# Transposing Q by DMA instead of on TensorE, in a fused attention and gated convolution kernel

## The chip, the cores and the metric

One core of a Trainium2 chip. The metric is the device time of one execution in microseconds. Times of a kernel are medians of several executions. Each run also has a profile, whose "span" is shorter than the time of the same execution (the profiled run of the kernel before took 229.07 us). The engines are TensorE (PE, with its weight loads PEld), VectorE (DVE), ScalarE (ACT), GpSimd (POOL) and SyncE (SP), which here issues every DMA. Ratios are computed as the mean time of one kernel's fast runs over that of the other's fast runs in the same rounds, so they are not quite the ratio of the medians quoted. In the experiments they leave out the profiled run; where that run was the fastest, slow runs are in the ratio, and the text says so. A single execution has the state "unknown" and no interval; such runs are used only where the difference is tens of microseconds.

## The reference

```python
B, H, S, D = 8, 8, 576, 64
scores = q @ k^T / sqrt(D)                       # per batch and head
cum    = cumsum(max(s, 0))                       # decay bias, per key and query
scores = where(causal, -1e9, scores + min(-(cum_q - cum_k), 0))
attn   = softmax(scores) @ v                     # -> x of shape (B, S, 512)
gate   = sigmoid(causal depthwise conv of x, 5 taps)
out    = (gate * (x @ w_val)) @ w_out
```

q, k and v are float32 with entries of about 0.1, so the scores are small.

## The kernel before

The kernel is one long list of tasks. A planner, run when the kernel is built, gives each task an engine and a place in that engine's queue, from a table of priorities (`DUE`), a table of engine choices (`CHOICE`) and assumed durations. Each engine then works through its own queue in that order. The scores need Q and K with the head dimension on the partitions, so both are loaded, cast to bf16 on GpSimd, transposed on TensorE into PSUM and copied out again by ScalarE or VectorE. Partition p of a load holds rows 4p to 4p+3, because that makes runs of 1 KB; the copy out of PSUM puts the rows in order again.

```python
def dma_qk(b, which, hs, dst):
    nc.sync.dma_start(out=dst, in_=src[b, hs, 0:512, :].rearrange("h (p j) d -> p h (j d)", j=4))

def qk_T(b, p):                                   # TensorE: 4 transposes of Q, 4 of K, for 2 heads
    for which in range(2):
        for j in range(4):
            nc.tensor.transpose(pt[:, which, j * 128:(j + 1) * 128],
                                qkbs[which][b % 2][:, j, p * 128:(p + 1) * 128], ident)

def qk_evac(e, b, p):                             # ACT or DVE, rows back in order
    copy[e](QKTs[b % 2][:, :, p, 0:512].rearrange("d w (x j) -> d w x j", j=4), ...)

def tap(n, sh):                                   # one convolution tap on VectorE, 4 of these per channel group
    nc.vector.scalar_tensor_tensor(gp[:, sh:S], x[:, 0:S - sh], cwT[:, c, 4 - sh:5 - sh], gp[:, sh:S], ALU.mult, ALU.add)

# in the planner, for every SyncE task:
if e == "SP":
    idle_at[e] = now + 0.06                       # SyncE is taken to be free again after 0.06 us
    dma_free = max(dma_free, now + 1.2) + us      # the DMA engines are busy for `us`
```

Of the kernel before, what the change touches and what calls it, by code (L numbers as in the profile page):

```python
# [9 lines left out]
FP32 = mybir.dt.float32  # L10
# [9 lines left out]
NKB = 5  # L20
# [184 lines left out]
def pcol(kb, qb):  # L205
    if kb == qb:
        return kb * 128
    if qb == 4:
# [16 lines left out]
DUE = dict(w=-9.02, lwv=-0.69, lwo=-0.63, cwv=-14.48, cwo=12.35, av=1.54, norm=-21.42, xt=-10.52, xe=-5.49,  # L225
           tap=4.19, dtap=-0.1, tanh=-21.1, val=6.51, dval=0.82, out=13.05, dout=0.32, oute=12.26,
           qt=-3.29, qe=62.47, tt=-0.65, te=-32.14, s4=-6.89, vp=-31.92, cast=41.14, lqk=-6.48,
           mask=-32.97, lv=-68.98)

STAY = (0.33, 20.6)  # L230

CHOICE = dict(cast="22212012",
              wts="00",
              te="10100110",
              qe="10010001000100000100100000000000",
              xe="01000110000001000110100110101101",
              tap0="10200210102212220121120122002000",
              oute="1010000010101000001000010000100000100000")


class Plan:
# [3 lines left out]
    LAG = 0.2  # L245
    SWITCH = 0.18
# [16 lines left out]
    def run(self):  # L263
# [33 lines left out]
        while len(self.order) < len(self.tasks):  # L297
            started, later = False, []
            for e in engs:
                if idle_at[e] > now + 1e-9:  # L300
                    later.append(idle_at[e])
                    continue
                pick = None
                for t in ready[e]:
                    at = can(t)
                    if at is None:
                        continue
                    if at > now + 1e-9:
                        later.append(at)
                        continue  # L310
                    key = t["key"] + (STAY[t["mode"] == "N"] if e == "PE" and t["mode"] != mode else 0)
                    if pick is None or (key, t["n"]) < pick[:2]:
                        pick = (key, t["n"], t)
                if pick is None:
                    continue
                t = pick[2]
                us = t["us"]
                if e == "PE" and t["mode"] != mode:
                    us += self.SWITCH
                    mode = t["mode"]  # L320
                for kind, tok in t["take"]:
                    if kind == "bank":

                        got = max((bank[i ^ 1], -i) for i in range(8) if bank[i] <= now + 1e-9)
                        self.slot[kind, tok] = i = -got[1]
                        bank[i] = NEVER
                    elif kind == "pair":
                        got = min((max(bank[i], bank[i + 1]), i) for i in range(0, 8, 2))
                        self.slot[kind, tok] = i = got[1]
                        bank[i] = bank[i + 1] = NEVER  # L330
                    else:
                        got = min(free[kind])
                        free[kind].remove(got)
                        self.slot[kind, tok] = got[1]
                t["start"] = now
                if e == "SP":
                    idle_at[e] = now + 0.06
                    dma_free = max(dma_free, now + 1.2) + us
                    t["done"] = dma_free + 0.8
                else:  # L340
                    idle_at[e] = t["done"] = now + us
                for kind, tok in t["give"]:
                    i, at = self.slot[kind, tok], t["done"] + self.LAG
                    if kind in ("bank", "pair"):
                        bank[i:i + (2 if kind == "pair" else 1)] = [at] * (2 if kind == "pair" else 1)
                    else:
                        free[kind].append((at, i))
                ready[e].remove(t)
                self.order.append(t)
                later.append(idle_at[e])  # L350
                started = True
                for o in after[t["n"]]:
                    o["at"] = max(o["at"], t["done"] + (self.LAG if o["eng"] != e else 0.0))
                    o["left"] -= 1
                    if o["left"] == 0:
                        ready[o["eng"]].append(o)
            if not started:
                assert later
                now = min(later)
# [3 lines left out]
def main_path(ctx, tc, q, k, v, s, moe_w_val, moe_conv_w, moe_w_out, out, okcnt):  # L363
# [39 lines left out]
    make_identity(nc, identf)  # L403
    vst = one.tile([128, NKB, 8, 65], FP32, name="vst")
# [14 lines left out]
    glus = two("glu", [128, 4, S], BF16)  # L419
    sp = one.tile([64, S], FP32, name="sp")  # L420
# [37 lines left out]
    for m, (nm, src, dst, sc) in enumerate((("wv", moe_w_val, wv, 1.0), ("wo", moe_w_out, wo, 0.5))):  # L458
# [3 lines left out]
        t = add("SP", 3.6, DUE["l" + nm], load, take=[("qkf", nm)])  # L462
# [57 lines left out]
    def qk_T(b, p):  # L520
        pt = slot["qt", b, p] = bank(("qt", b, p), 128, 1024, BF16).rearrange("d (w s) -> d w s", w=2)
        for which in range(2):
            for j in range(4):
                nc.tensor.transpose(pt[:, which, j * 128:(j + 1) * 128],  # L524
                                    qkbs[which][b % 2][:, j, p * 128:(p + 1) * 128], ident)

    def qk_evac(e, b, p):
        copy[e](QKTs[b % 2][:, :, p, 0:512].rearrange("d w (x j) -> d w x j", j=4),  # L528
                       slot["qt", b, p].rearrange("d w (j x) -> d w x j", j=4))
# [33 lines left out]
    def mask(n, hh):  # L563
        d = slot["Pt", n][:, hh, 0:512].rearrange("k (g q) -> k g q", g=4)
        nc.gpsimd.affine_select(out=d, in_=d, pattern=[[0, 4], [1, 128]], compare_op=ALU.is_ge, fill=0.0, base=0,  # L565
                                channel_multiplier=-1)
# [15 lines left out]

    def norm(n):
        b, p = divmod(n, 4)
        pv = slot["av", n][:, :, 0:NKB * 65].rearrange("t h (g d) -> t h g d", d=65)
        nc.vector.reciprocal(recs[:, n], pv[:, :, :, 64])
# [3 lines left out]
    def x_T(n):  # L590
        b, p = divmod(n, 4)
        pt = slot["x", n] = bank(("x", n), 128, S, BF16)
        slot["g", n] = work("gp", n, [128, S], FP32)
        for i in (4, 0, 1, 2, 3):
            nc.tensor.transpose(pt[:, WIN[i]:WIN[i] + 128], xns[b % 2][:, i, p * 128:(p + 1) * 128], ident)  # L595
# [4 lines left out]

    def tap0(e, n):
        b, c = divmod(n, 4)
        scaled(e, slot["g", n], xTs[b % 2][:, c, :] if e == "POOL" else slot["x", n], cwT[:, c, 4:5])
# [39 lines left out]
    for b in range(B):  # L643
# [3 lines left out]
        if b == 0:  # L647
            t_tl = add("SP", 1.6, -8.4, lambda: load_tail(0))
            t_tail = T["tailc", 0] = add("DVE", 0.45, -6, lambda: nc.vector.tensor_copy(tailbs[0], tails[0]), [t_tl])
            for p in range(4):  # L650
                for wh in range(2):
# [3 lines left out]
                    t = add("SP", 0.95, -8.5 + 0.5 * p + wh * 0.01, ld)  # L655
                    T["cast", 0, wh, p] = add(("DVE", "ACT", "POOL"), (0.32, 0.5, 0.8), p - 9, lambda e, p=p, wh=wh: cast_qk(
                        copy[e], 0, wh, HP[p], slot["f", 0, wh, p]), [t], pick=("cast", 2 * p + wh))
                t = add("SP", 1.4, -8.3 + 0.5 * p, lambda p=p: load_v_pair(p))
                T["vp", 0, p] = add("DVE", 0.85, p - 2, lambda p=p: vprime(nc.vector, 0, p), [t, t_w])
        else:  # L660
            fs = []
            for wh in range(2):
                def ld(b=b, wh=wh):
                    f = slot["f", b, wh] = work("qkf", (b, wh), [128, 8, 256], FP32)
                    dma_qk(b, wh, slice(0, 8), f)
                t = add("SP", 3.8, n0 + DUE["lqk"], ld, take=[("qkf", (b, wh))])
                c = add("POOL", 1.95, n0 + DUE["cast"], lambda b=b, wh=wh: cast_qk(
                    nc.gpsimd.tensor_copy, b, wh, slice(0, 8), slot["f", b, wh]),
                    [t] + [T.get(("qt", b - 2, p)) for p in range(4)], give=[("qkf", (b, wh))])
                for p in range(4):  # L670
                    T["cast", b, wh, p] = c
            t = add("SP", 1.6, n0 + DUE["lqk"] + 0.5, lambda b=b: load_tail(b), [T.get(("tailc", b - 2))])
            t_tail = T["tailc", b] = add("POOL", 0.7, n0 + DUE["cast"] + 0.3, lambda b=b: nc.gpsimd.tensor_copy(
                tailbs[b % 2], tails[b % 2]), [t, T.get(("tt", b - 2))])
            ts = [add("SP", 1.7, n0 + DUE["lv"] + i * 0.01, lambda b=b, i=i: load_v_block(b, i),
                      [T["vp", b - 1, p] for p in range(4)]) for i in range(NKB)]
            for p in range(4):
                T["vp", b, p] = add("POOL", 1.4, n0 + p + DUE["vp"], lambda b=b, p=p: vprime(nc.gpsimd, b, p),
# [7 lines left out]
        for p in range(4):  # L686
            t = T["qt", b, p] = add("PE", 0.45, n0 + p + DUE["qt"] if b else p - 6.9, lambda b=b, p=p: qk_T(b, p),
                                    [T["cast", b, 0, p], T["cast", b, 1, p]] + old_s, take=[("bank", ("qt", b, p))])
            T["qe", b, p] = add(("ACT", "DVE"), (0.9, 1.15), n0 + p + DUE["qe"] if b else p - 6.8,
                                lambda e, b=b, p=p: qk_evac(e, b, p), [t], give=[("bank", ("qt", b, p))], pick=("qe", n0 + p))  # L690

        e4 = {}
        for ps_ in ([[p] for p in range(4)] if b == 0 else [[0, 1, 2, 3]]):
# [3 lines left out]
                [t_te] + [T["qe", b, p] for p in ps_] + [T.get(("av", b - 2, p)) for p in range(4)],  # L697
# [6 lines left out]
        for p in range(4):  # L704
            n = n0 + p
            es = []
            for i in range(3):
                take = [("pair", ("s", n, i))] + ([("P", n)] if i == 0 else [])
                t = T["s", n, i] = add("PE", 0.26, n + 0.3 * i, lambda n=n, i=i: scores(n, i),
                                       [T["qe", b, p], t_te if i else None, T.get(("s", n, i - 1)), T.get(("s", n - 1, 2))],  # L710
                                       take=take, mode="R")
                t = add("ACT", 0.905, n + 0.3 * i, lambda n=n, i=i: exps(n, i), [t], give=[("pair", ("s", n, i))])
                es += [t] if i else [add("POOL", 0.58, n + DUE["mask"] + 0.01 * hh, lambda n=n, hh=hh: mask(n, hh), [t])
# [5 lines left out]
            t = T["norm", n] = add("DVE", 0.94, n + DUE["norm"], lambda n=n: norm(n), [t], give=[("pair", ("av", n))])  # L719
# [5 lines left out]
            t = T["tap0", n] = add(("ACT", "DVE", "POOL"), (0.63, 0.73, 1.55), n + DUE["tap"],  # L725
                                   lambda e, n=n: tap0(e, n), [t, t_cw], pick=("tap0", n))
            for sh in range(1, 5):
# [15 lines left out]
        for i in range(NKB):  # L743
# [6 lines left out]
            add("SP", 0.95, n0 + DUE["oute"] + DUE["dout"] * i, lambda b=b, i=i: store(b, i), [t], give=[("ot", (b, i))])  # L750
# [81 lines left out]
```

## Time and profile before

| | before |
|---|---|
| time, median | 228.57 us (228.2 to 228.89) |
| span | 227.2 us |
| DVE / ACT / PE / POOL busy | 192.5 / 176.2 / 174.9 / 138.6 us |
| DMA queue's share of 16 engines | 66.7% |
| mean granted TensorE clock | 0.985 |

An engine's busy time is a lower bound for the span; what is above it is idle time, and the question is always which engine has least of it, and where. The lines themselves are shown in the prediction. One view is SyncE's own queue. These lines are its timeline over one batch in the middle of the kernel before. Columns: start, time from the first issue of the row to the end of its last, engine and line, operation, data, number of DMAs.

```profile
103.63 5.35 SPq L507 DMA_DIRECT2D vst<-in_v_dram  x5
109.08 0.56 SPq L482 DMA_DIRECT2D qkf<-in_q_dram  x1
109.74 1.02 SPq L482 DMA_DIRECT2D qkf<-in_k_dram  x1
110.85 1.44 SPq L482 DMA_DIRECT2D qkf<-in_q_dram  x1
113.44 4.59 SPq L641 DMA_DIRECT2D out_dram<-ot  x3
```

On average SyncE has room: its 129 issues sum to 111.5 us of 227. But 42.0 us of these fall in the first 45 us; from 80 to 210 us they are 45.8 us of 130.

### The profile page before, as it was taken

To read this page: it belongs to the slowest core of one execution; us is meant where nothing else is said; L and a number is where in the kernel's file an instruction comes from. 1 tells how busy PE (TensorE), PEld (TensorE's weight loads), DVE (VectorE), ACT (ScalarE), POOL (GpSimd) and SP (SyncE) were. 2 spreads that over 40 slices of the span, in tenths; PEclk is the share of its full clock that TensorE was granted. 3 is DMA by queue.
4 is the path that set the end of the run, shared out by engine and by line. 5 is a ranking of instruction groups with operands and counts; after the bars stand their busy time and mean duration, and the time that the engine had idled before them with its cause. 6 is when DMAs were issued, how large, how long until landed. Compare 5 with 4: busy or idle time off the path is not lost. (4 is left out here: it accounts for less than half of the span.)

```text
span 227.2 us, 5999 instructions
## 1 busy us (share of the span) xinstructions
PE 174.9 (77%) x2392; PEld 117.6 (52%) x2411; DVE 192.5 (85%) x319; ACT 176.2 (78%) x229; POOL 138.6 (61%) x154
## 2 busy tenths in 40 slices
PE   0777667768576987798877988896998999999750
PEld 0555453455443664467545654675566555656320
DVE  3546989699999597999999899999999999999900
ACT  2395989954598599985999979899999799966330
POOL 5374574599264995799987876885945775200000
PEclk9999996999999999999999999999999999999996
DMA  4999889999996299907994683159229123034351
GB/s 137 245 278 305 245 160 258 315 228 207 312 307 166 60 196 364 301 12 173 233 346 178 137 246 114 41 130 153 92 95 220 50 83 94 3 132 157 128 190 35
DMA packets 69230, 40.48 MB, mean 178 GB/s; under 512 B 47109, under 2 KB 63493, under 8 KB 69194
## 3 DMA queue, kind: packets, MB, share of 16 engines
q1 hardware_dynamic: 69194, 40.01, 66.7%
q8 instruction: 21, 0.34, 0.7%
q14 instruction: 15, 0.12, 0.2%
HBM read 30.57 MB, written 9.44 MB: 176 GB/s over the span
## 5 line engine op out<-in xcount | busy, mean ns | idle before, releaser
L609 DVE SCALAR_TENSOR_TENSOR gp<-banks,cwT,gp 128x575 f32<-128x575 bf16 (+3 forms) x128 | 103.5, 812 | 3.2 <-ACT gp L395 0.3
L559 ACT ACTIVATE P<-banks 128x1024 bf16<-128x1024 f32 x96 | 95.1, 1030 | 11.7 <-PE banks L533 11.1
L565 POOL TENSOR_SCALAR_AFFINE_SELECT P<-P 128x512 bf16<-128x512 bf16 x64 | 40.4, 653 | 36.4 <-ACT P L559 36.2
L533 PE MATMUL banks<-QKT 64*128 64x128 bf16 (+4 forms) x576 | 39.5, 250 | 15.6 <-ACT P L559 6.3
L621 PE MATMUL banks<-xT,wv 128*128 128x288 bf16 x256 | 40.6, 288 | 5.0 <-DVE gp L609 3.0
L633 PE MATMUL banks<-wo,glu 128*128 128x512 bf16 x141 | 37.6, 379 | 4.7 <-DVE glu L627 1.1
L580 PE MATMUL banks<-Vp,P 128*128 128x65 bf16 x960 | 35.8, 196 | 2.8 <-POOL Vp L495 1.3
L580 PEld LDWEIGHTS <-P 128*128 128x128 bf16 x960 | 33.7, 99 | 6.4 <-issue 3.3
L533 PEld LDWEIGHTS <-QKT 64*128 64x128 bf16 x576 | 19.2, 97 | 31.7 <-issue 25.6
L495 POOL TENSOR_TENSOR Vp<-vst,w 128x650 bf16<-128x650 f32 x28 | 35.3, 1282 | 0.0
L621 PEld LDWEIGHTS <-wv 128*128 128x128 bf16 x256 | 23.0, 98 | 17.1 <-issue 10.3
L528 ACT COPY QKT<-banks 128x1024 bf16<-128x1024 bf16 x26 | 26.1, 1019 | 5.4 <-PE banks L524 5.1
L627 DVE SCALAR_TENSOR_TENSOR glu<-th,banks 128x288 bf16<-128x288 f32 x64 | 27.1, 447 | 3.2 <-PE banks L621 2.7
L614 ACT ACTIVATE th<-gp 128x576 f32<-128x576 f32 x32 | 22.1, 692 | 9.2 <-DVE gp L609 9.0
L587 DVE TENSOR_TENSOR xn<-banks,recs 128x640 bf16<-128x640 f32 x32 | 26.4, 825 | 1.1
L638 ACT COPY ot<-banks 128x512 f32<-128x512 f32 (+1 forms) x31 | 18.1, 587 | 9.6 <-PE banks L633 6.0
L397 POOL TENSOR_SCALAR gp<-xT,cwT 128x576 f32<-128x576 bf16 x12 | 20.7, 1725 | 7.3 <-ACT xT L599 4.1
L633 PEld LDWEIGHTS <-glu 128*128 128x128 bf16 x160 | 14.6, 97 | 18.2 <-issue 5.0
L595 PE MATMUL banks<-ident,xn 128*128 128x128 bf16 x160 | 14.6, 223 | 6.3 <-DVE gp L609 2.8
L595 PEld LDWEIGHTS <-xn 128*128 128x128 bf16 x160 | 9.9, 99 | 12.7 <-DVE xn L587 5.0
L524 PE MATMUL banks<-ident,qb 128*128 128x128 bf16 x128 | 13.2, 230 | 2.1 <-DVE glu L627 0.7
L485 POOL CAST qb<-qkf 128x2048 bf16<-128x2048 f32 x7 | 13.2, 1891 | 2.3 <-DMA qkf<-in_q_dram 2.3
(56 smaller groups left out, 148.5 us busy)
## 6 DMA issues: line engine op xcount, KB each, us to landing
out_dram<-ot SPq DMA_DIRECT2D x32, 256.0 KB, 2.1
qkf<-in_q_dram SPq DMA_DIRECT2D x7, 1024.0 KB, 9.3
qkf<-in_k_dram SPq DMA_DIRECT2D x7, 1024.0 KB, 8.8
vst<-in_v_dram SPq DMA_DIRECT2D x28, 256.0 KB, 5.0
vst<-in_v_dram SPq DMA_DIRECT2D x15, 128.0 KB, 4.5
first<-in_q_dram SPq DMA_DIRECT2D x4, 256.0 KB, 3.3
first<-in_k_dram SPq DMA_DIRECT2D x4, 256.0 KB, 3.5
tail<-in_q_dram SPq DMA_DIRECT2D x8, 128.0 KB, 8.8
```

What stands on the lines that cost most here:

```text
L495: eng.tensor_tensor(Vps[b % 2][:, :, h], vst[:, :, h], w[:, :, b * 8 + 2 * p:b * 8 + 2 * p + 2].unsqueeze(3).to_broadcast([128, NKB, 2, 65 ...
L528: copy[e](QKTs[b % 2][:, :, p, 0:512].rearrange("d w (x j) -> d w x j", j=4), slot["qt", b, p].rearrange("d w (j x) -> d w x j", j=4))
L533: nc.tensor.matmul(ps[:, hh, c0:c0 + nq], QKTs[b % 2][r, 1, p, k0:k0 + 128], QKTs[b % 2][r, 0, p, q0:q0 + nq], **kw)
L559: nc.scalar.activation(out=slot["Pt", n][:, :, step * 512:(step + 1) * 512], in_=slot["s", n, step], func=AF.Exp, scale=0.125)
L565: nc.gpsimd.affine_select(out=d, in_=d, pattern=[[0, 4], [1, 128]], compare_op=ALU.is_ge, fill=0.0, base=0, channel_multiplier=-1)
L580: nc.tensor.matmul(ps[:, hh, qb * 65:qb * 65 + 65], lhsT, Vps[b % 2][:, kb, 2 * p + hh, :], start=(kb == 0), stop=(kb == qb))
L587: nc.vector.tensor_tensor(xns[b % 2][:, :, p * 128:(p + 1) * 128].rearrange("t g (h d) -> t h g d", h=2), pv[:, :, :, 0:64], recs[:, n].un ...
L595: nc.tensor.transpose(pt[:, WIN[i]:WIN[i] + 128], xns[b % 2][:, i, p * 128:(p + 1) * 128], ident)
L609: nc.vector.scalar_tensor_tensor(gp[:, sh:S], x[:, 0:S - sh], cwT[:, c, 4 - sh:5 - sh], gp[:, sh:S], ALU.mult, ALU.add)
L621: nc.tensor.matmul(ps, wv[:, dc, c * 128:(c + 1) * 128], xTs[b % 2][:, dc, o:o + 288], start=(dc == 0), stop=(dc == 3))
L627: nc.vector.scalar_tensor_tensor(glus[b % 2][:, c, o], slot["t", n][:, o], 1.0, slot["v", n, hf], ALU.add, ALU.mult)
L633: nc.tensor.matmul(ps, glus[b % 2][:, c, WIN[i]:WIN[i] + 128], wo[:, c, :], start=(c == 0), stop=(c == 3))
```

## The change

Its intent is to take the transposition of Q off TensorE and its copy out of PSUM off ScalarE and VectorE. The changed kernel lets a DMA transpose the bf16 data while it moves it, and the DMA engines had time left in the second half. Batch 0 stays on TensorE. As it is used here, a DMA transpose writes its rows to neighbouring columns and does not put rows 4p+j back in order; each one therefore takes 32 partitions of one j, and the 128 queries of a block stay in the order (j, p). The causal mask and the identity of a later transpose are permuted to match. Two smaller parts come along: the second convolution tap may go to GpSimd, and GpSimd taps are written as products of two tensors. All priorities and choices were searched anew; the planner's assumed durations changed a little, and the reciprocal of the softmax sums became a task of its own.

```diff
+QPE = (0,)                                        # batches whose Q stays on TensorE
+    def q_dma(b, i):
+        for j in range(4):
+            c = i * 128 + j * 32
+            nc.sync.dma_start_transpose(out=QKTs[b % 2][:, 0, :, c:c + 32], in_=qkbs[0][b % 2][i * 32:(i + 1) * 32, j, :])
...
+            qd = [add("SP", 0.6, n0 + DUE["qd"], lambda b=b, i=i: q_dma(b, i), [T["cast", b, 0, 0]] + old_s) for i in range(4)]
...
-        d = slot["Pt", n][:, hh, 0:512].rearrange("k (g q) -> k g q", g=4)
-        nc.gpsimd.affine_select(out=d, in_=d, pattern=[[0, 4], [1, 128]], ...
+        d = slot["Pt", n][:, hh, 0:512].rearrange("k (g j x) -> k g j x", g=4, j=4)
+        nc.gpsimd.affine_select(out=d, in_=d, pattern=[[0, 4], [1, 4], [4, 32]], ...
...
+    def product(n, sh, out):
+        nc.gpsimd.tensor_tensor(out, xTs[b % 2][:, c, 0:S - sh], cwT[:, c, 4 - sh:5 - sh].to_broadcast([128, S - sh]), ALU.mult)
+    def tap_either(e, n, sh):
+        if e == "DVE":
+            return tap(n, sh)
+        product(n, sh, tmp[:, sh:S])
+        nc.gpsimd.tensor_tensor(gp[:, sh:S], gp[:, sh:S], tmp[:, sh:S], ALU.add)
...
-DUE = dict(w=-9.02, ...)   CHOICE = dict(cast="22212012", ...)
+DUE = dict(w=18.95, ...)   CHOICE = dict(cast="10210201", ..., tap1="00100010010000001000110010011010")
```

The 0.6 in the added task: the planner takes four DMA transposes to need 0.6 us of the DMA engines.

## The prediction

> **What bounds the kernel now.** I read the page first (engine shares, slices, chain), then the busy times in four stretches, then the groups of instructions, then the waits and the DMA issues.
>
> ```profile
> PE 174.9 (77%) x2392; PEld 117.6 (52%) x2411; DVE 192.5 (85%) x319; ACT 176.2 (78%) x229; POOL 138.6 (61%) x154
> DMA  4999889999996299907994683159229123034351
> ```
>
> VectorE (DVE) is busiest, ScalarE (ACT) and TensorE (PE) close behind, GpSimd (POOL) has room. The DMA row is nearly full for the first third and thin after. The chain of waits has collapsed to the last eviction (0%) and says nothing, so the stretches must carry the argument. Columns: length, then busy time of PE, weight loads, DVE, ACT, POOL, then clock, DMA share, GB/s.
>
> ```profile
> 0.00:20.00 20.00, 10.69 (x116) 7.90 (x118) 9.12 (x15) 10.69 (x15) 10.07 (x24) 1.00 0.88 229
> 20.00:80.00 60.00, 43.97 (x652) 30.08 (x651) 52.89 (x84) 45.16 (x57) 40.67 (x42) 0.97 0.93 231
> 80.00:210.00 130.00, 112.52 (x1594) 76.13 (x1607) 124.80 (x209) 116.28 (x152) 87.83 (x89) 1.00 0.57 154
> 210.00:228.00 18.00, 7.68 (x40) 3.53 (x39) 5.73 (x14) 4.05 (x7) 0.00 (x0) 0.88 0.34 114
> ```
>
> From 80 to 210 us DVE works 124.80 of 130 us, 96%: that stage is bound by DVE's sum of work. ACT at 89% is a close second and would bind if DVE alone were relieved. DVE idles 10.9 us in the first 20 us (inputs arriving), 7.1 in 20 to 80 (DMA 93% busy, so loads pace part of it), 5.2 in the middle, and 11.5 of the last 17.2 (the last projection and stores). In all 227.2 - 192.5 = 34.7 us.
>
> The groups whose durations I use (count, then busy us, mean ns):
>
> ```profile
> L609 DVE SCALAR_TENSOR_TENSOR gp<-banks,cwT,gp 128x575 f32<-128x575 bf16 (+3 forms) x128 | 103.5, 812 | 3.2 <-ACT gp L395 0.3 <-POOL gp L397 0.3
> L528 ACT COPY QKT<-banks 128x1024 bf16<-128x1024 bf16 x26 | 26.1, 1019 | 5.4 <-PE banks L524 5.1
> L528 DVE COPY QKT<-banks 128x1024 bf16<-128x1024 bf16 x6 | 7.3, 1218 | 0.4 <-ACT P L559 0.4
> L524 PE MATMUL banks<-ident,qb 128*128 128x128 bf16 x128 | 13.2, 230 | 2.1 <-DVE glu L627 0.7 <-DVE xn L587 0.6 <-DVE QKT L528 0.3
> L495 POOL TENSOR_TENSOR Vp<-vst,w 128x650 bf16<-128x650 f32 x28 | 35.3, 1282 | 0.0
> L397 POOL TENSOR_SCALAR gp<-xT,cwT 128x576 f32<-128x576 bf16 x12 | 20.7, 1725 | 7.3 <-ACT xT L599 4.1 <-DVE xT L599 2.9
> ```
>
> The convolution taps (L609) are over half of DVE's work. The evictions of transposed Q and K (L528) cost 33.4 us over ACT and DVE.
>
> **What the Trainium skill says.** "VectorE: DVE Perf Modes", section "The three transpose paths", gives 390 ns for a 128x128 bf16 transpose on TensorE and 1309 ns by the DMA crossbar. Here a PE transpose takes 230 ns busy, less than its figure; no DMA transpose is in this trace. "Advanced Engine Details and Errata", "X-Bar Transpose (TRN2)", says such DMAs are as fast as ordinary ones, 350 to 400 GB/s expected; this kernel's ordinary traffic ran at 154 to 231 GB/s in the long stretches. "DMA: Bandwidth & Descriptors", "Rules for kernel authors", warns that transfers under 64 KB pay mostly overhead; each new transpose is 32 rows x 512 x 2 B = 32 KB. The trace leans that way in latency: of the V loads, 32 KB pieces took 3.2 us to land and 128 KB pieces 4.5. "Trainium Kernel Development and Optimization", "Key Constraints": GpSimd cannot access PSUM. The trace agrees: on POOL the tap reads xT in SBUF, on DVE the PSUM bank. So a tap moved to POOL must wait for xT's copy.
>
> **The change part by part.** The diff does three things: Q by DMA; a second convolution tap that may go to POOL, and POOL taps written as a product of two tensors; and a new order and engine choice for every task. I count choices from the strings.
>
> PE: 7 batches x 16 Q transposes vanish: 112 x 0.230 = 25.8 us, to about 149. K keeps its 16 a batch. The permuted identity undoes the query order at no extra instruction.
>
> ACT: evictions of whole width fall from 26 to 11: -15 x 1.02 = -15.3. First taps 12 to 8: -4 x 0.75 = -3.0. xT copies 13 to 18: +5 x 0.65 = +3.3. Output evictions 31 to 35: +4 x 0.59 = +2.4. One weight cast (+1.9, my estimate from POOL's 1.89 for the same shape), one input cast and one tail +1.2. Sum -9.5: 176.2 to 166.7.
>
> DVE: second taps on POOL, 10 x 0.81 = -8.1. Output evictions 9 to 5, -2.7; xT copies 19 to 14, -2.3; weight cast -1.2; tail -0.4. Against it: first taps 8 to 10, +1.6; two more input casts, +1.3; evictions 6 x 1.22 = 7.3 become 3 x 1.22 plus batch 0's eight halves at about 0.61, 8.5, so +1.2. Sum -10.6: 192.5 to about 182.
>
> POOL: a product of 576 elements, scaled from the V' row, is 1282 x 576/650 = 1.14 us in place of 1.725. First taps 12 x 1.725 = 20.7 become 14 x 1.14 = 15.9, -4.8. Each moved second tap is product plus add, 2 x 1.14 us: 10 x 2.27 = +22.7. Three fewer casts of about 0.8, -2.4; the permuted identity about +0.3. Sum +15.8: 138.6 to about 154. The mask keeps its 512 elements; I leave it at 0.65 us in spite of its deeper pattern.
>
> DMA: a batch of Q is 512 KB, 2048 packets if they are 256 B each. The 256-byte packets in the trace records of this kernel last 21.7 ns on average (976 us for 45,056): 2048 x 21.7 / 16 engines = 2.8 us a batch, 19 us in all; the queue's share goes from 66.7% (151.5 us) to about 171 us. Of the path to Q, the wait is slack: the last Q cast ended at 138 us and its transposes ran at 173 us, so several microseconds of landing time lie beside other work. Issue: SyncE took 0.4 to 0.6 us for an ordinary small issue; 16 of these cost some 8 us of its queue a batch. In steady state it issues about 10 us of other DMAs per batch of some 27 us (130 us hold about 4.8 batches), so it fits.
>
> On the path: in the DVE-bound middle the gain is DVE's, not PE's 25.8 or ACT's 9.5; those two keep ACT from binding in its place. 182 busy + 34.7 idle = 216.7 span. Time is 1.4 us over span (228.57 against 227.2): 218. The re-fitted task order may trim a microsecond or two of early idle, the DMA's full first 80 us may cost as much: transposes of batches 1 and 2 fall there, 2 x 2.8 us of a queue already at 93%. I settle at 217.
>
> **The rivals.** (1) The crossbar transposes are latency-bound: at the skill's 1.31 us each in series, 16 make 21 us a batch on top of about 17 us (0.65 of 27) of other DMA. That exceeds the batch's 27 us; the DMA would bind and the time would be 250 us or more. For it: 32 KB pieces[...]. Against: ordinary DMAs overlap freely here, 256-byte packets take 22 ns, and the landing time is likely most of that 1.31. (2) SyncE's issue becomes the bound or blocks at its head: transposes wait for the cast and for the scores of two batches before, and loads and stores behind them wait too. SyncE spent the whole of 0 to 45 us issuing without rest. If batch 1's Q comes 5 to 8 us late, DVE starves once: 222 to 226. (3) POOL becomes part of the path: the mask already waits 36.2 us for the exponentials, and 2.3 us tap pairs in front of masks hold up attention and then DVE; at 154 of about 215 us it is 72% busy. Cost some 3 to 5 us: 220 to 222. (4) PE and ACT relief shortens early idle as well, since both wait in turn with DVE there: 211 to 213.
>
> **Range and chances.** Centre 217; 210 if rival 4 holds and the new order packs better, 226 if rivals 2 and 3 bite together. Over 2% faster means under 224.0: I give 0.79. Within 2%: 0.11. Slower, almost only rival 1: 0.10.
>
> **What would show it.** Right: DVE busy 180 to 184, ACT 165 to 169, PE about 149, POOL 152 to 158; DVE at 95% or more from about 80 us to the tail; L528-type evictions 14 of full width and 8 halves; DVE idle near 35 us; queue share below 85%; transposes landing within about 6 us of issue. Wrong: long SyncE waits ahead of loads, TensorE waiting for DMA at the scores, DVE idle above 42 us, or DMA at 90% throughout. A POOL product far from 1.14 us, or masks well over 0.65, would break POOL's sum; a tap on DVE slower than 0.81 while POOL is busier would break DVE's.

## The result, and the profile after

The changed kernel takes 326.38 us (median of 4, 325.79 to 326.9) against 228.73 in the same rounds: 1.424 times as long, with a 95% interval of 1.4137 to 1.4342. The result is right.

These lines are from the page of the kernel after: busy times, and in 40 slices of the span the busy tenths of each engine, the granted clock, the DMA share, and the rate in GB/s.

```profile
PE 187.7 (58%) x2299; PEld 122.3 (38%) x2299; DVE 177.1 (55%) x307; ACT 167.9 (52%) x222; POOL 160.5 (49%) x174
...
DVE  4699402794800570368703940397018963998950
...
PEclk9999555897655895658756985599657995999996
DMA  6999118998115911996119212991158119322342
GB/s 156 278 290 194 31 24 221 239 286 173 28 24 157 287 24 24 217 252 201 28 27 275 54 24 80 359 229 27 28 160 152 26 25 194 136 63 76 122 152 90
...
q1 hardware_dynamic: 87114, 43.70, 53.1%
```

VectorE and ScalarE have less to do than before, TensorE (187.7 us against 174.9) and GpSimd (160.5 against 138.6) more, and none is above 58%. The engines' sums do not explain 98 us; the engines are waiting. The DMA row shows the pattern: stretches at nine tenths alternate with stretches at one tenth, where the rate falls to 24 to 31 GB/s, and towards the end of most of these VectorE falls to nothing. The DMA engines are as idle there as the others.

The timeline of SyncE says what those stretches are:

```profile
78.34 20.79 SPq L551 DMA_TRANSPOSE QKT<-qb  x16
99.17 1.52 SPq L493 DMA_DIRECT2D qkf<-in_k_dram  x1
...
108.63 21.60 SPq L551 DMA_TRANSPOSE QKT<-qb  x16
130.27 0.58 SPq L493 DMA_DIRECT2D qkf<-in_k_dram  x1
130.96 8.26 SPq L518 DMA_DIRECT2D vst<-in_v_dram  x5
```

Sixteen transposes hold SyncE for about 21 us, and nothing else is issued meanwhile. The instructions on the transposed tile give the price of one, as minimum, median and maximum in ns, and the time from issue to landing:

```profile
L551 SPq DMA_TRANSPOSE QKT<-qb x112: 1177/1236/2722, 27.7 to 267.2; - x112
...
DMA to landing us min/median/max: 2.3/2.3/7.2
```

So 1.24 us of issue each, 143.9 us for the 112 by the trace's records, while the 129 plain issues sum to 122.3 us. With the short gaps between issues (219 of under 0.2 us, 13.5 us in all) SyncE is occupied for 280 of 325 us. So with these issue times no order of the tasks could bring the change near 228 us: even with the 111.5 us of plain issues of the kernel before, the sum is 255 us. One transpose moves 128 packets of 256 bytes (and 32 of 4 bytes), which at the 21.7 ns of the prediction is, as an estimate, 0.17 us of the 16 engines: the moving takes a seventh of the issuing. That is why the DMA share is a tenth and the rate 32 KB per 1.3 us, 25 GB/s.

The stretch between the first two of these blocks, and the second block (the columns are those of the prediction):

```profile
49.10:78.30 29.20, 23.05 (x279) 15.17 (x280) 19.16 (x32) 19.09 (x25) 20.53 (x20) 0.79 1.04 243
78.30:99.10 20.80, 4.76 (x31) 2.50 (x29) 7.06 (x12) 2.19 (x4) 9.46 (x9) 0.58 0.21 39
```

And TensorE's timeline inside the second block and just after it, with the wait before each row in brackets:

```profile
90.06 0.29 PE L555 MATMUL banks<-QKT 64*128 64x128 bf16 x2 [3.90 <-DMA QKT<-qb]
95.28 0.29 PE L555 MATMUL banks<-QKT 64*128 64x128 bf16 x2 [4.93 <-DMA QKT<-qb]
101.53 0.29 PE L555 MATMUL banks<-QKT 64*128 64x128 bf16 x2 [5.97 <-DMA QKT<-qb]
```

The scores of a batch go block by block, and each block of queries comes with one group of four transposes, 5 to 6 us after the last. TensorE has 0.29 us of work per block and waits for the rest. Its queue is in order, so the projections behind the scores wait too. The list of waits names both halves, Q that comes late and loads and stores that stand behind the transposes in SyncE's queue:

```profile
ACT P L581 <- PE banks L555: 66.5, 18, 15.2
...
PE banks L555 <- DMA QKT<-qb: 49.9, 11, 6.0
...
ACT ot L678 <- DMA out_dram<-ot: 41.7, 7, 16.7
...
POOL kb L496 <- DMA qkf<-in_k_dram: 33.9, 3, 16.8
```

(Columns: who waited for whom, us in total, times, longest.) ScalarE waited 41.7 us for an output buffer whose store was behind transposes, and GpSimd 33.9 us for a K load.

### The profile page after: what moved, and what is told of

Its sections match the earlier page's. It is cut to its first block, busy times and chain, and to the rows that moved or that the text cites. A ratio compares the mean times of both kernels' runs of the same rounds, so it can differ in the third digit from the quotient of the medians.

```text
span 324.9 us, 5970 instructions
## 1 busy us (share of the span) xinstructions
PE 187.7 (58%) x2299; PEld 122.3 (38%) x2299; DVE 177.1 (55%) x307; ACT 167.9 (52%) x222; POOL 160.5 (49%) x174
## 3 DMA queue, kind: packets, MB, share of 16 engines
q1 hardware_dynamic: 87114, 43.70, 53.1%
## 5 line engine op out<-in xcount | busy, mean ns | idle before, releaser
L649 DVE SCALAR_TENSOR_TENSOR gp<-banks,cwT,gp 128x572 f32<-128x572 bf16 (+3 forms) x118 | 93.2, 803 | 12.1 <-POOL gp L629 7.5
L555 PE MATMUL banks<-QKT 64*128 64x128 bf16 (+4 forms) x576 | 45.4, 274 | 60.3 <-DMA QKT<-qb 49.9
L587 POOL TENSOR_SCALAR_AFFINE_SELECT P<-P 128x512 bf16<-128x512 bf16 x64 | 45.4, 732 | 43.7 <-ACT P L581 43.7
L661 PE MATMUL banks<-xT,wv 128*128 128x288 bf16 x256 | 46.6, 324 | 30.1 <-ACT ot L678 23.8
L678 ACT COPY ot<-banks 128x512 f32<-128x512 f32 (+1 forms) x35 | 20.6, 592 | 50.6 <-DMA out_dram<-ot 41.7
L602 PEld LDWEIGHTS <-P 128*128 128x128 bf16 x960 | 37.5, 105 | 21.0 <-DVE ot L678 14.8
L661 PEld LDWEIGHTS <-wv 128*128 128x128 bf16 x256 | 25.5, 107 | 43.7 <-issue 34.7
L496 POOL CAST kb<-qkf 128x2048 bf16<-128x2048 f32 x7 | 13.3, 1893 | 33.9 <-DMA qkf<-in_k_dram 33.9
L625 DVE COPY xT<-banks 128x576 bf16<-128x576 bf16 x14 | 6.3, 451 | 26.7 <-PE banks L620 26.7
L592 POOL TENSOR_SCALAR_AFFINE_SELECT P<-P 128x512 bf16<-128x512 bf16 (+1 forms) x11 | 6.5, 590 | 26.5 <-ACT P L567 26.5
L629 POOL TENSOR_TENSOR gp<-xT,cwT 128x576 f32<-128x576 bf16 x14 | 16.1, 1148 | 0.3 <-ACT xT L625 0.3
L643 POOL TENSOR_TENSOR gp<-gp,tmp 128x575 f32<-128x575 f32 x10 | 14.0, 1402 | 2.7 <-DVE gp L404 2.1
```

What stands on the lines that cost most here:

```text
L496: eng(qkbs[which][b % 2].rearrange("p j (h d) -> p h j d", h=8)[:, hs], f.rearrange("p h (j d) -> p h j d", j=4))
L555: nc.tensor.matmul(ps[:, hh, c0:c0 + nq], QKTs[b % 2][r, 1, p, k0:k0 + 128], QKTs[b % 2][r, 0, p, q0:q0 + nq], **kw)
L587: nc.gpsimd.affine_select(out=d, in_=d, pattern=[[0, 4], [1, 4], [4, 32]], compare_op=ALU.is_ge, fill=0.0, base=0, channel_multiplier=-1)
L602: nc.tensor.matmul(ps[:, hh, qb * 65:qb * 65 + 65], lhsT, Vps[b % 2][:, kb, 2 * p + hh, :], start=(kb == 0), stop=(kb == qb))
L661: nc.tensor.matmul(ps, wv[:, dc, c * 128:(c + 1) * 128], xTs[b % 2][:, dc, o:o + 288], start=(dc == 0), stop=(dc == 3))
```

## The experiments

The theory (A): each DMA transpose costs a fixed time of the queue that issues it, A1, or a time by the number of 16-row by 128-column pieces in it, A2. The rivals: the rest of the change is at fault (B), any sixteen dependent DMAs at this place would do it (C), transposes in flight hold up all other DMA traffic, as if the crossbar that the prediction names blocked it for everybody (D). Two cautions. First, the comparison with the reference passed for every run below, even for those whose Q is wrong, because the scores are so small that attention is nearly uniform; it does not guard Q. The versions called right below were also compared in a functional simulation with q and k ten times larger: the kernel before, the changed one and these versions all differ from the reference by a relative 0.0044, the wrong-order one by 0.72. Second, the median of the kernel before lay between 228.6 and 230.3 us in the rounds of different runs, so small differences are read from the ratios.

**Is it the transposes, or the rest of the change?**

```diff
-QPE = (0,)
+QPE = tuple(range(8))
```

> The changed kernel with Q of all eight batches transposed on TensorE, everything else of the change kept (task order, second tap on GpSimd, interleaved query order). Theory A (the cost is SyncE's issue of the DMA transposes, 112 x 1.24 us, which holds its queue about 21 us a batch): the whole 98 us go away, time 220 to 232, SyncE's plain issues about 110 us in sum, granted clock back near 0.98. Rival B (the new task order or the taps and masks on GpSimd cost a good part of it): time stays above 245.

Measured: 236.95 us, ratio 1.0414 to the kernel before (1.0276 to 1.0552); plain issues 115.7 us in sum, clock 0.958. Two of the four runs are slow; the two fast ones, 234.48 and 235.7 us, are 2.8% above the fast ones of the kernel before (mean 228.6). So some 90 of the 98 us go with the DMA transposes, and B falls as the main cause. But the time is 3 to 5 us above the range expected, so the rest of the change is no gain in this form. That its order does not suit a kernel with all of Q on TensorE is likely, and not shown.

**A price per instruction, or per piece?** Two runs keep bytes and pieces and change only how many instructions carry them.

```diff
 # four_big: 4 instructions of 128 rows x 512 columns, 32 pieces each; wrong query order on purpose
-        for j in range(4):
-            c = i * 128 + j * 32
-            nc.sync.dma_start_transpose(out=QKTs[b % 2][:, 0, :, c:c + 32], in_=qkbs[0][b % 2][i * 32:(i + 1) * 32, j, :])
+        nc.sync.dma_start_transpose(out=QKTs[b % 2][:, 0, :, i * 128:(i + 1) * 128], in_=qkbs[0][b % 2][:, i, :])
 # half_size: 32 instructions of 32 rows x 256 columns, 4 pieces each; right result
+            for g in (0, 2):
+                nc.sync.dma_start_transpose(out=QKTs[b % 2][:, 0, g:g + 2, c:c + 32],
+                                            in_=qkbs[0][b % 2][i * 32:(i + 1) * 32, j, g * 128:g * 128 + 256])
```

> Four DMA transposes of 128 rows a batch in place of 16 of 32 rows: same bytes and same 128-column pieces, wrong query order on purpose, so a wrong result. If the 1.24 us are a fixed price of an instruction (theory A1): issue of about 1.2 us each, 5 us a batch, time 225 to 240. If the price goes with the bytes or the pieces of 16 rows x 128 columns (theory A2, 8 pieces now, 32 then): about 4.8 us each, 20 us a batch, time 315 to 335.

> Thirty-two DMA transposes of 32 rows x 256 columns a batch in place of 16 of 32 x 512: same bytes, right result. Theory A1 (fixed price of an instruction): 1.24 us each, 42 us a batch, time above 430. Theory A2 (price by pieces, 4 now): about 0.65 us each, 21 us a batch and a little more for the gaps, time 320 to 350.

The same line of the view of the tile as above, first of four_big, then of half_size:

```profile
L549 SPq DMA_TRANSPOSE QKT<-qb x28: 1207/1223/2636, 26.6 to 160.6; - x28
```

```profile
L552 SPq DMA_TRANSPOSE QKT<-qb x224: 1159/1230/2387, 26.1 to 409.9; - x112
```

| transposes a batch | pieces each | median issue | time |
|---|---|---|---|
| 4 | 32 | 1.223 us | 227.1, later 228.16 us |
| 16 (the change) | 8 | 1.236 us | 326.38 us |
| 32 | 4 | 1.230 us | 470.46 us |

The median issue time does not move over a factor of eight in size. (The means are 1.45, 1.29 and 1.25 us; a few transposes take up to 2.7 us, and among 28 they weigh more.) A1 holds, and A2, which asked for 4.8 us at 32 pieces, is refuted. Between the rows, one more transpose costs (470.46 - 326.38) / 112 = 1.29 us and (326.38 - 228.16) / 84 = 1.17 us of the whole kernel: almost the full issue time lies on the path. Up to four a batch it is far less, about 0.25 us each, as a run without any shows below. (The time of 470.46 us is that of a single run.)

The second run of four_big, timed:

> The kernel with four DMA transposes of 128 rows a batch once more, now timed: its one run took 227.1. Theory A1 (5 us of SyncE a batch): 225 to 229, so within 2% of the kernel before, and 2 to 6 us above the kernel without any Q transposition.

Measured: 228.16 us, ratio 1.0084 (0.9976 to 1.0193); two of the four runs are slow, and the two fast ones, 224.8 and 227.37 us, are at 0.998 of the kernel before. Either way it is as fast as the kernel before. Cutting the number of instructions to a quarter gives back the whole loss, but brings no gain.

**Would any DMA do it?**

```diff
-            nc.sync.dma_start_transpose(...)      # 16 a batch
+            nc.sync.dma_start(out=QKTs[b % 2][i * 32:(i + 1) * 32, 0, j, 0:512], in_=qkbs[0][b % 2][i * 32:(i + 1) * 32, j, :])
```

> The 16 DMA transposes a batch replaced by 16 plain DMA copies of the same 32 rows x 512 columns inside SBUF, wrong result on purpose. Theory A (transposing issue is what is dear): 0.4 to 0.6 us each, 6 to 10 us a batch, time 225 to 250. Rival C (any 16 dependent DMAs of 32 KB at this place cost as much, through queueing or landing): time above 300.

Measured: 257.97 us, issue 0.588 us in the median. C as stated (above 300) is refuted, but the time is 8 us above what theory A expected. Sixteen plain copies hold SyncE 10 to 13 us a batch in its timeline and are not free either. This run has about the issue price that the prediction assumed, and even then the kernel is 28 to 29 us slower than before, and 37 us slower than the run without any transposition below.

**Whose time is it, the queue's or the crossbar's?**

```diff
-            nc.sync.dma_start_transpose(
+            nc.scalar.dma_start_transpose(
```

> The changed kernel with its 112 DMA transposes issued from ScalarE's queue in place of SyncE's, same order of tasks. If the 1.24 us are time of the issuing sequencer (theory A1), they move to ScalarE: its 168 us of work plus 112 x 1.3 us make at least 313 us, so time 310 to 340, and SyncE's plain DMAs go on meanwhile at 100 GB/s or more. If instead the crossbar blocks the DMA rings for everybody (rival D), plain traffic in those stretches stays at 25 to 45 GB/s as in the changed kernel.

Measured: 362.0 us. The price moves with the queue. ScalarE's timeline in this run:

```profile
25.11 21.13 ACTq L551 DMA_TRANSPOSE QKT<-qb  x16
46.29 0.68 ACT L654 ACTIVATE th<-gp 128x576 f32<-128x576 f32 x1 [20.18 <-DMA QKT<-qb]
```

For 21 us ScalarE computes nothing. Busy times in two stretches inside that block:

```profile
30.00:34.00 4.00, 0.00 (x0) 0.00 (x0) 0.00 (x0) 0.00 (x0) 0.00 (x0) 0.50 0.12 25
40.00:44.00 4.00, 0.00 (x0) 0.00 (x0) 0.00 (x0) 0.00 (x0) 0.00 (x0) 0.50 1.11 306
```

From 40 to 44 us, while ScalarE goes on issuing transposes, a weight load that SyncE issued at 38.2 runs, and the rate is 306 GB/s: in this run transposes in flight did not hold up plain traffic, and D falls. From 30 to 34 there is none, because SyncE itself was waiting: its list of waits in this run puts 16.0 us of waiting before weight loads down to DMA transposes, and 155 us in all kinds of issue. Both queues share their completion counters in this program (by the trace, the first weight load waits for a counter that two of the transposes raise). The run came out above the range I had given (310 to 340), and for this reason it is not a clean measure of what ScalarE's queue would cost.

**Is it harmless where the queue has room?**

```diff
-QPE = (0,)
+QPE = tuple(range(7))                             # only the last batch by DMA
```

> Only the last batch's Q by DMA transpose, in 16 pieces, the other seven on TensorE. Theory A1: its 21 us of issue fall where SyncE has only stores and one batch of V left, so little of it is on the path: time within 2% of the run with all of Q on TensorE (232 to 242 us). If every batch by DMA cost the average (326 - 237) / 7 = 12.7 us, 245 to 253.

Measured: 249.47 us, ratio 1.0884 (1.0706 to 1.1062): 12.5 us more than with none by DMA, the average price of a batch. My reading of A1 was wrong here. The timeline of SyncE:

```profile
152.50 8.23 SPq L681 DMA_DIRECT2D out_dram<-ot  x4
160.82 22.58 SPq L551 DMA_TRANSPOSE QKT<-qb  x16
```

The last Q cast ended at 136.1 us. The transposes stand behind four stores in the queue, which wait for ScalarE's output, start 25 us later and end at 183.4. What waited for them shows in two more lines, one of the list of waits and one of TensorE's timeline:

```profile
ACT ot L678 <- DMA out_dram<-ot: 12.7, 4, 10.5
187.43 0.61 PE L555 MATMUL banks<-QKT 64*128 64x320 bf16 x4 [10.29 <-ACT P L581]
```

TensorE's wait of 10.29 us ends with ScalarE's exponentials, and ScalarE had stood 10.5 us, until 185.87, for an output buffer. The store that frees it was issued at 183.50, right behind the sixteenth transpose. So in this run the long wait came from what stands behind the block, and a late Q is not seen in it. A queue with idle time on average is no help when it is in order: a block of 22 us delays everything behind it.

**Is it only the order of issue?**

```diff
-                    idle_at[e] = now + 0.06
+                    idle_at[e] = now + (5.25 if us == 0.6 else 0.6)
```

> The changed kernel with its task order planned again after telling the planner that SyncE is held 5.25 us by each group of four DMA transposes, so that loads and stores are issued between the groups. If SyncE's sum is the bound (122 us of plain issue + 144 us of transposes + gaps of some 17 us, and waits): 290 to 335, no better than 290. If only the bad placing of the 21 us blocks cost the time: below 270.

Measured: 352.62 us, worse than the change. The edit did not do what it was meant to: the planner still put the transposes in blocks of 16, once of 32 (44 us), probably because of their high priority. Below 270 was not reached, and the time is above the other range too. A good interleaving was not tried, so this run says little; that even the best order could not come below some 255 us follows from the sum of issues given above. How much of the loss beyond that is bad order stays open.

**What could the change gain if Q cost nothing?**

```diff
 def q_dma(b, i):
-        for j in range(4): ... nc.sync.dma_start_transpose(...)
+        pass                                      # wrong on purpose; Q of odd batches set to zero once
```

> The changed kernel with its DMA transposes left out altogether, same order of tasks (Q stays zero for odd batches and stale for even ones, wrong on purpose): what the change could gain if Q's transposition were free. If the prediction's sum for VectorE held (182 us busy + 35 us idle): 214 to 220. If the rest of the change keeps VectorE's idle time near the 49 us of the kernel with four transposes a batch: 222 to 228.

Measured: 221.06 us, ratio 0.9728 (0.9592 to 0.9865). It falls between the two ranges expected. So with the order and the engines of the change, a free transposition is worth about 3%; the 217 of the prediction was out of reach even then. Four transposes a batch use this up: by the medians 228.16 - 221.06 = 7.1 us for 28 of them, about 0.25 us each, with a few microseconds of noise in the difference.

**Has GpSimd become part of the path?** On four_big:

```diff
 def tap_either(e, n, sh):
-        if e == "DVE":
-            return tap(n, sh)
+        return tap(n, sh)                         # all second taps on VectorE
```

> The kernel with four DMA transposes a batch (wrong query order), the ten second taps done on VectorE at the same places of the order. If GpSimd has become part of the path (the third rival of the prediction): time equal or up to 4 us lower than 227. If VectorE's sum of work binds: 8 us of VectorE work come back, 232 to 237.

Measured: 231.01 us, ratio 1.0101 (0.9972 to 1.023). The time lies in neither range expected, and against four_big's 1.0084 the difference is within the intervals. VectorE's busy time rose from 176.5 to 183.4 us and GpSimd's fell from 160.5 to 136.4, and the time hardly moved. The third rival is not supported, nor is VectorE's sum as the sole bound: inconclusive.

**Right versions with few transposes.** To have a block of 128 queries in one transpose and in order, Q must be loaded with row i*128+p on partition p, in runs of 256 bytes:

```diff
-        nc.sync.dma_start(out=dst, in_=src[b, hs, 0:512, :].rearrange("h (p j) d -> p h (j d)", j=4))
+            for i in range(4):                    # Q only
+                nc.sync.dma_start(out=dst[:, :, i * 64:(i + 1) * 64], in_=src[b, hs, i * 128:(i + 1) * 128, :].rearrange("h p d -> p h d"))
 # q_dma as in four_big; mask and identity as in the kernel before
```

> A version with a right result: Q loaded in natural order of rows (four loads a batch in runs of 256 bytes), so that a whole block of 128 queries is one DMA transpose, four a batch, plain mask and identity. Theory A1: issue of SyncE per batch falls from 21 us to about 5 for the transposes plus 4 for the loads: time 222 to 236. Masks fall from 0.74 to about 0.65 us if the deeper pattern was the reason, and stay if sharing with VectorE was. Rival E: the 256-byte loads and transposes fill the DMA (above 90%) and time is above 236.

Measured: 248.02 us, ratio 1.089. A1's range missed, rival E's time met, though not by its mechanism as put: the queue's share was 82.0%, not above 90. That is an average; by stages the DMA share was 1.08 from 20 to 80 us, where four_big had 1.10, and 0.88 from 80 to 210 us against 0.82. SyncE's plain issues rose from 120.9 us in sum in four_big to 141.6. Which of the two costs the 20 us was not separated. The four loads took 3.2 to 7.6 us of SyncE a batch by its timeline in the first 90 us, mostly more than the 4 I had allowed. One clear answer: the mask took 0.642 us here against 0.732 with the pattern of the change, so the deeper pattern was the reason.

Last, transposing only the last four batches that way, with SyncE's measured issue times in the planner and a fresh search of the order from that of the kernel before; and a control with the same planner and no DMA transposes, whose table of priorities and choices stays close to that of the kernel before.

```diff
+QPE = (0, 1, 2, 3)                                # control: tuple(range(8))
-                    idle_at[e] = now + 0.06
-                    dma_free = max(dma_free, now + 1.2) + us
+                    dma_free = max(dma_free, now + t["iss"] + 0.7) + us
+                    idle_at[e] = max(now + t["iss"], dma_free - 7.0)
 # iss: 1.31 a transpose, 0.6 a Q or K load, 4.3 for Q in four loads, 1.05 a V load, 1.35 the tail pair
```

> Control: the task order of the kernel before, nearly unchanged, with all of Q on TensorE, natural query order, and the first taps on GpSimd as products. Expected within 2% of the kernel before: 224 to 230. It says what the next run's order search is worth without any DMA transpose.

> Right result: Q of the last four batches only by DMA, four transposes of 128 rows a batch, Q loaded there in natural order in four loads, a task order searched for it with SyncE's issue times in the planner. Theory A1: about 10 us of SyncE a batch where it has room, 64 transposes less on TensorE and 8 evictions less on ScalarE and VectorE: 220 to 227, 0 to 3% below the kernel before. Rival: the order of issue again ties scores to SyncE's queue: above 230.

Measured: control 219.1 us, ratio 0.960 (0.9528 to 0.9671); the last four batches by DMA 217.85 us, ratio 0.9534 (0.9462 to 0.9605). All their runs, 217.31 to 220.22 us, lie below all runs of the kernel before in these rounds, 226.86 to 232.1. The intervals overlap, so a gain from the sixteen DMA transposes is not shown; the two tables differ in much else. What is shown is that nearly all of the gain comes without them. The control lies below the range expected for it. Which of its differences does it, the GpSimd taps as products or the new order, was not separated.

## Why the prediction was wrong

The main step that failed is a term of the sum: "Issue: SyncE took 0.4 to 0.6 us for an ordinary small issue; 16 of these cost some 8 us of its queue a batch." A plain issue was taken as the measure of a transposing one. It took 1.24 us and, with the gap, 1.3; sixteen took 21 us. The conclusion "so it fits" fell with it: 21 us and its own 10 us of other DMAs are more than the 27 us of a batch (over the whole changed kernel the plain issues are 15 us a batch). The runs with 4, 16 and 32 instructions show that this price is paid per instruction.

The second failing step is "Of the path to Q, the wait is slack." The 35 us were read from the end of the cast to the last transposes of the last batch. In the kernel before, TensorE's first transpose of a batch followed the end of its Q cast after 2.8, 5.0, 2.6, 22, 3.2, 4.2 and 20 us in batches 1 to 7, so the slack was mostly small. And in the changed kernel Q stands in an in-order queue: the first DMA transpose of a batch was issued 2 to 40 us after the end of the cast, 31 in the median (it also needs the scores of two batches before; the record does not separate the two), the last one 21 us later, and TensorE waited 49.9 us in all for it at the scores, a sign of being wrong that the prediction had named. And the plain copies show that even at half the price 28 us are lost: the first step alone, corrected in size only, does not explain everything.

The first rival had the right 21 us a batch and the right consequence ("250 us or more"), but put it on the DMA engines, which were a tenth busy; the second rival named the right queue and sized it at 5 to 8 us once. Together they were the answer; the prediction gave 0.10 to a slower kernel. That the first rival's 21 us agree with the 21 us measured is partly luck: it took a figure for another shape, and as DMA time. The argument against it, that landing time is most of that figure, failed: here the issue alone took 1.24 us. The transfer term was right: the queue's share of 53.1% of 324.9 us is 172.5 us, against about 171 predicted. That number was the wrong one to ask for. A small misreading: the 1.4 us between span and time mix two executions; the profiled one took 1.9 us more than its span.

The sums of work, step by step:

| | predicted | measured | why |
|---|---|---|---|
| ACT | 166.7 | 167.9 | right |
| DVE | about 182 | 177.1 | below the 180 to 184 given: batch 0's casts took 0.43 us, not 0.66, taps 0.80, and half of the halves 0.41 |
| POOL | about 154 | 160.5 | mask 0.73 in place of 0.65 us (64 of them, 5 us); the adding half of a moved tap 1.40, not 1.14 (10, 2.6 us); the product 1.15, right |
| PE | about 149 | 187.7 | 112 transposes less, but nearly all others longer: for 128x288, 324 ns against 288, at a mean granted clock of 0.781 against 0.985; some 3 us of the difference are matmuls of the last projection that the trace before lacks (141 records of 160) |

The mean clock was lowest in the runs that waited most (0.696 in half_size, 0.745 with ScalarE issuing), but not only in the blocks: in the changed kernel it was 0.79 in the stretch before the block shown, 0.58 in the block, 0.55 in the 9.5 us after it, and 0.85 in the block from 178 to 199 us. I take it as a companion rather than the cause; no run separates the two.

Last, "182 busy + 34.7 idle" assumed that VectorE's idle time stays. In the changed kernel it is 147.8 us. With four transposes a batch, where issue is no longer the bound, it is 223.1 - 176.5 = 46.6 us; these are the stretches of e2b_four_big, to be held against those in the prediction:

```profile
20.00:80.00 60.00, 44.83 (x609) 30.98 (x613) 46.06 (x77) 43.01 (x55) 49.34 (x50) 0.80 1.10 246
80.00:210.00 130.00, 114.16 (x1528) 75.79 (x1538) 117.19 (x205) 111.92 (x150) 102.78 (x102) 0.95 0.80 178
```

VectorE idles 13.9 us from 20 to 80 (7.1 before) and 12.8 from 80 to 210 (5.2 before). Subtracting work from the busiest engine of a packed schedule gave an upper bound of the gain, not the gain. What takes the place of that work was not settled; the run without any Q transposes shows only that part of it is there without them.

## What to carry to other kernels

Before work is moved to DMA, count the instructions and ask what one of them costs the queue that issues it; bytes and the share of the DMA engines say nothing about that. An in-order queue has to be judged by the time from the moment its data is ready to the last piece issued, with everything that stands ahead, and by what stands behind: in the run with one batch by DMA, it was the stores behind the block that stopped ScalarE. A planner should be given the issue times; here it assumed 0.06 us (one attempt to correct that did not break up the blocks). If a DMA must transpose, give each instruction as much as the layout allows: against no transposition at all, four of 128x512 a batch cost about 7 us here and sixteen of 32x512 about 105.

## What the Trainium skill lacked or had wrong

- "VectorE: DVE Perf Modes", "The three transpose paths", gives 1309 ns for a 128x128 transpose by DMA and does not say whether the time goes with the size. Here the spacing of transposes was about 1.3 us for 32x512, and the issue was 1.22 to 1.24 us for 4, 8 or 32 pieces of 16x128: a price of the instruction, and of the issuing queue. One of 128x512 also took 1.22 us to issue (landing in 2.4 us at best, 4.3 in the median).
- "Advanced Engine Details and Errata", "X-Bar Transpose (TRN2)", says that such DMAs are as fast as ordinary ones, at 350 to 400 GB/s. In instructions of 32 KB they ran at 25 GB/s here; four of 128 KB issued in 5.17 us are, as an estimate, at most about 100 GB/s. That section lacks the issue time.
- "DMA: Bandwidth & Descriptors", "Issuing engines are not separate DMA queues", calls the sequencer's time to initiate a DMA "usually small relative to the DMA itself". For a 32 KB transpose it was 1.24 us, against an estimated 0.17 us of moving and 2.3 us from issue to landing, and for the plain 32 KB copies 0.59 us.
- The same page's rule ("Rules for kernel authors") that transfers under 64 KB pay mostly overhead held for the 32 KB transposes. The rule does not say how much of the overhead is time of the issuing engine: with ScalarE issuing sixteen of them, ScalarE computed nothing for 21 us.
- No page that I found gives the cost of a GpSimd select by its pattern: 128x512 bf16 took 0.642 us with two levels and 0.732 with three.
